# A delta rule and a SoLU layer in one kernel: an issue order for all engines written by hand, the first recurrence on GpSimd, weights on VectorE, 1/norm by Newton steps, softmax a step later

## The chip, the cores and the metric

The kernel runs on one core of one Trainium2 chip. The metric is device time in microseconds (us) of one execution. The engines are TensorE (PE in the profile, its weight loads PEld), VectorE (DVE), ScalarE (ACT), GpSimd (POOL) and SyncE (SP, which issues DMAs). Each works through its own queue in order, and they meet through semaphores.

## The reference

Inputs: q, k, v of shape (4 batches, 8 heads, 768 positions, 48), beta of shape (4, 8, 768), and the weights of a SoLU layer.

```python
k_n = k / (norm(k) + 1e-6)
state = zeros(B, H, D, D)
for t in range(768):
    y[t] = q[t] @ state
    v_old = state.T @ k_n[t]
    state = state + beta[t] * outer(k_n[t], v[t] - v_old)
x = y as (3072 tokens, 384)
h = x @ w_in                                  # 1024 columns
e = exp(h - max(h));  solu = h * e / (sum(e) + 1e-9)
ln = (solu - mean) / sqrt(var + 1e-6) * g_ln
out = ln @ w_out                              # 384 columns
```

## The kernel before

The delta rule is worked in chunks of 64 positions. A unit (bp, s, c2) is one pair of batches (bp), one of six blocks of 128 positions (s) and one half of it (c2): 24 units, walked by the loop `for n in range(N + 3)` with s outermost and bp innermost, so that the state of a pair of batches is used in every second step. For each block s, the four units' 32 x 32 Gram matrices are inverted together, with one matrix a partition: `inv_step` does a multiply (L269) and an add (L273) for each of 30 columns, on DVE for s = 0 and on POOL for the others. This is the recurrence ("rec s" below). It needs the Gram matrices (`gram_p` on PE, L180 and L183, copied by ACT, L196, and through DRAM and back by `to_inv`, tile gd and then ginv), the norms of the keys (`norms`, with a power on POOL, L224) and `inv_begin`. `inv_end` sends the inverse through DRAM into zt and gx (for s = 0 by DVE transposes, L278 and L280), and `tlevel_a`/`tlevel_b` (PE L309, L325; ACT L316, L331) join the 32-blocks to 64.

One step n of the chain: `chain_bank` (PE L352, state times k and q; DVE L354), `chain_ups` (PE L366, ACT L368), `chain_kpu` (PE L381 and L383; DVE L390 adds to the state, ACT L392 copies y). Behind the chain comes the layer: `moe_x` transposes y of unit n-1 and splits it in two f16 parts (PE L402, ACT L405, DVE L406), `moe_h` multiplies with w_in (18 matmuls, L415) and does the softmax and the normalization (DVE maximum L421, ACT exp L424, DVE product L426, ACT square L430, DVE L431 to L433, POOL power L434 and L435, ACT L436), `moe_p` transposes unit n-2 (PE L446, ACT L448, DVE L449) and `moe_o` multiplies unit n-3 with w_out (24 matmuls, L459).

PSUM holds one buffer for bank, ups and kpu in turn (tag "ch"), one for yps, one for h, two for Gram and tlevel work (tag "g") and two for the layer's other work. The weights come as 64-bit floats and are turned to two f16 parts by `split_w` (L94 to L102), w_in with POOL's help and w_out on DVE.

The order on PE is the order of the program, under this line; the other engines' instructions are put in order by a scheduler with a model of their costs:

```python
with tc.manual_schedule(engines={mybir.EngineType.PE}):
```

Of the kernel before, what the change touches and what calls it, by code (L numbers as in the profile page):

```python
# [622 lines left out]
```

## Time and profile before

| | us |
|---|---|
| median of 3 runs (lowest, highest) | 655.91 (655.41, 658.05) |
| the profiled execution | 655.79 |
| its span, first to last instruction | 654.1 |
| PE / DVE / ACT / POOL busy | 452.3 / 260.5 / 236.5 / 280.9 |
| mean granted clock of TensorE | 0.778 of 2.4 GHz |

In the rows that follow, a time is counted from the first instruction of the span. The granted clock is given as a share of 2.4 GHz; it takes two levels here, 1.00 (2.4 GHz) and 0.50 (1.2 GHz), so a value between them is a mix over the stretch. "A <- B" in a wait means that A's engine sat idle until B was done.

### The profile page before, as it was taken

The page shows a single profiled execution, that of the slowest core. Times are in us where ns is not written, and L with a number is a line of the kernel's source. Part 1 is how long each engine was busy: PE and PEld are TensorE (multiplying, and loading weights), DVE is VectorE, ACT ScalarE, POOL GpSimd, SP SyncE. Part 2 cuts the span into 40 slices and gives each one's busy share as a digit, 9 for nine tenths or more (in the row PEclk, how much of TensorE's full clock was granted, in tenths as well). Part 3 has the DMA queues.
Part 4 walks back from the last instruction along what each step waited for, and adds up shares of the span by engine and source line. Part 5 has one row for each costly group of instructions (what it writes and reads, how often), then busy time and mean ns, then how long its engine had stood idle before and what let it go on. Part 6 is the DMA issues. An engine that isn't in the chain of part 4 may idle for free.

```text
span 654.1 us, 18470 instructions
## 1 busy us (share of the span) xinstructions
PE 452.3 (69%) x8248; PEld 312.5 (48%) x8248; DVE 260.5 (40%) x516; ACT 236.5 (36%) x442; POOL 280.9 (43%) x418
## 2 busy tenths in 40 slices
PE   6430033819487869769859669848768888998975
PEld 5430033616354546536646446625445555655543
DVE  1789999121530432313441232343123332223341
ACT  2232152333332433243434244333153443424342
POOL 5786357864785038840048830068810000000000
PEclk9755555567697797777788788968967889878898
DMA  7963430128113532234232244311060000000000
GB/s 212 298 166 122 88 106 27 66 82 144 59 39 106 134 62 63 74 99 121 74 47 66 71 111 110 82 37 43 34 149 2 14 15 13 15 13 14 13 14 24
DMA packets 78159, 49.52 MB, mean 76 GB/s; under 512 B 64768, under 2 KB 67968, under 8 KB 78080
## 3 DMA queue, kind: packets, MB, share of 16 engines
q1 hardware_dynamic: 74624, 43.63, 25.9%
q10 hardware_dynamic: 3456, 4.72, 2.1%
q8 instruction: 64, 1.05, 0.7%
q14 instruction: 15, 0.12, 0.1%
HBM read 33.13 MB, written 15.20 MB: 74 GB/s over the span
## 4 chain that ended last, share of the span: by engine, by line
issue 42%; POOL 32%; DVE 11%; DMA 8%; SPq 4%; ACT 2%; PE 1%; POOLq 0%; DVEq 0%
POOL y L273 11%; POOL itmp L269 11%; POOL nn L224 3%; DVE y L273 3%; DMA ginv<-gd 3%; DVE itmp L269 2%; POOL y L254 2%; POOL st L434 2%; POOL v L243 2%; SPq L138 1%; DMA g_sb<-g_ln_dram 1%; DMA gd<-g 1%; SPq L209 1%; DMA kq<-kq_dram 1%; POOL y L255 1%
## 5 line engine op out<-in xcount | busy, mean ns | idle before, releaser
L434 POOL TENSOR_TENSOR st<-st,nhalf 128x1 f32<-128x1 f32 x24 | 13.2, 549 | 244.2 <-DVE st L433 244.2
L421 DVE TENSOR_REDUCE st<-h 128x1 f32<-128x1024 f32 x24 | 29.4, 1224 | 184.7 <-PE h L415 184.7
L352 PE MATMUL bank<-st,kq 48*64 48x48 f32 x704 | 39.5, 284 | 82.9 <-DVE st L390 69.6
L273 POOL TENSOR_TENSOR y<-y,itmp 128x30 f32<-128x30 f32 (+9 forms) x150 | 78.1, 521 | 10.9
L269 POOL TENSOR_TENSOR itmp<-y,ginv 128x30 f32<-128x30 f32 (+9 forms) x150 | 73.6, 490 | 10.8
L352 PEld LDWEIGHTS bank<-st,kq 48*64 48x64 f32 x704 | 36.3, 199 | 87.5 <-issue 72.5
L180 PE MATMUL p<-kq 48*64 48x64 f32 x768 | 48.8, 307 | 28.9 <-ACT pt L187 19.2
L459 PEld LDWEIGHTS <-ph 128*128 128x128 f16 x384 | 47.6, 124 | 42.9 <-issue 28.3
L459 PE MATMUL ops<-wout_hi,ph 128*128 128x384 f16 x192 | 57.8, 472 | 2.2 <-DVE st L422 1.1
L180 PEld LDWEIGHTS p<-kq 48*64 48x64 f32 x768 | 44.6, 216 | 30.2 <-ACT pt L187 19.9
L224 POOL TENSOR_TENSOR nn<-ginv,half 128x32 f32<-128x32 f32 x6 | 32.8, 5461 | 53.4 <-DMA ginv<-gd 47.1
L426 DVE SCALAR_TENSOR_TENSOR pr<-h,e 128x1024 f32<-128x1024 f32 x24 | 29.4, 1224 | 54.7 <-ACT e L424 54.7
L309 PE MATMUL mps<-zt,gx 32*32 32x32 f32 x768 | 19.2, 206 | 45.5 <-DVE zt L278 30.7
L436 ACT ACTIVATE pr<-pr,st 128x1024 f32<-128x1024 f32 x24 | 29.8, 1241 | 56.8 <-POOL st L435 56.8
L406 DVE TENSOR_TENSOR xl<-xps,xh 128x384 f16<-128x384 f32 x24 | 13.4, 557 | 84.7 <-ACT xh L405 84.4
L415 PEld LDWEIGHTS <-xh 128*128 128x128 f16 x288 | 28.4, 105 | 36.8 <-issue 11.0
L352 PE MATMUL yps<-st,kq 48*64 48x48 f32 x704 | 38.8, 285 | 9.1 <-ACT yo L392 9.1
L331 ACT COPY zt<-mps 32x256 f32<-32x256 f32 x48 | 17.4, 362 | 75.6 <-PE mps L325 75.3
L183 PE MATMUL g<-kq 48*64 48x64 f32 x640 | 38.4, 308 | 5.8 <-DVE pt L190 3.7
L415 PE MATMUL h<-win_hi,xh 128*128 128x512 f16 x144 | 41.4, 431 | 0.9 <-ACT xh L405 0.9
L430 ACT ACTIVATE e<-pr,st 128x1024 f32<-128x1024 f32 x24 | 27.6, 1149 | 39.2 <-DVE st L429 37.6
L352 PEld LDWEIGHTS yps<-st,kq 48*64 48x64 f32 x704 | 35.4, 199 | 9.4 <-ACT yo L392 9.4
(99 smaller groups left out, 990.5 us busy)
## 6 DMA issues: line engine op xcount, KB each, us to landing
kq<-kq_dram SPq DMA_DIRECT2D x40, 192.0 KB, 5.1
gd<-g SPq DMA_DIRECT2D x10, 512.0 KB, 2.8
v<-vn_dram SPq DMA_DIRECT2D x12, 384.0 KB, 4.5
k<-kn_dram SPq DMA_DIRECT2D x12, 384.0 KB, 3.8
out_dram<-o ACTq DMA_DIRECT2D x24, 192.0 KB, 1.9
wi<-w_in_dram SPq DMA_DIRECT2D x6, 512.0 KB, 7.2
wo<-w_out_dram SPq DMA_DIRECT2D x8, 384.0 KB, 3.1
ginv<-gd SPq DMA_DIRECT2D x20, 128.0 KB, 3.8
```

The costliest lines, as they stand in the source:

```text
L180: nc.tensor.matmul(out=ps[o : o + C, h], lhsT=k[lan, 0, h], rhs=k[lan, 1, h], start=True, stop=True)
L183: nc.tensor.matmul(out=gp[o : o + C, h], lhsT=k[lan, 0, h], rhs=k[lan, 0, h], start=True, stop=True)
L224: nc.gpsimd.tensor_tensor(out=n, in0=gi.rearrange("p j i -> p (j i)")[:, 0 : 32 * 32 : 33], in1=half, op=ALU.pow)
L269: eng.tensor_tensor(out=tv, in0=y[:, 0:j, j : j + 1].to_broadcast([P, j, n]), in1=b[:, j : j + 1, j + 1 : 32].to_broadcast([P, j, n]), op= ...
L273: eng.tensor_tensor(out=y[:, 0:j, j + 1 : 32], in0=y[:, 0:j, j + 1 : 32], in1=tv, op=ALU.add)
L352: nc.tensor.matmul(out=ps[o : o + C, h], lhsT=k[lan, i, h], rhs=sb[lan, h], start=i == 0 or h == 0, stop=i == 0)
L415: nc.tensor.matmul(out=hps[:, 512 * q : 512 * q + 512], lhsT=a[:, k], rhs=b[:, k, 512 * q : 512 * q + 512], start=j == 0, stop=j == len(pa ...
L421: nc.vector.tensor_reduce(out=nmax, in_=hps, op=ALU.max, axis=AX.X, negate=True)
L426: nc.vector.scalar_tensor_tensor(out=pr, in0=hps, scalar=1.0, in1=e, op0=ALU.mult, op1=ALU.mult, accum_out=sp,)
L430: nc.scalar.activation(e, pr, AF.Square, bias=mean, scale=1.0, accum_out=ss)
L436: nc.scalar.activation(pr, pr, AF.Identity, bias=mean, scale=rr)
L459: nc.tensor.matmul(out=ops, lhsT=a[:, k], rhs=b[:, k], start=i == 0, stop=i == 23)
```

## The change

All five engines now issue in the order of the program text, which is written out anew, for the stretch ahead of the loop and for each step. The loads stand first, in an order of their own. `inv_step` works on POOL for every s, and the loop takes rec s in three steps of ten columns, half of them at the step's start and half later, where it took two steps of fifteen. `inv_begin` becomes `inv_bm`, `inv_ya` and `inv_yb`. `norms` has no power on POOL: it takes 1/norm from an integer guess and three Newton steps on DVE. The weights are converted by DVE and ACT alone, with one DVE operation fewer, the last eight slices inside steps 0 to 2. The softmax of unit n-2 stands in step n, where `moe_h` of the same unit ran in step n-1; the last three of nine passes of `moe_h` go to the step's end, and `chain_kpu` stands ahead of `moe_p`. The output's DMA goes from ACT's queue to SP's. Buffers change by one here and there (pt 10 to 11, raw weights and pr 4, ginv 2, u and r 1).

```diff
-    p3 = ctx.enter_context(tc.tile_pool(name="p3", bufs=3))
+    pw = ctx.enter_context(tc.tile_pool(name="pw", bufs=4))
-    pm = ctx.enter_context(tc.tile_pool(name="pm", bufs=10))
+    pm = ctx.enter_context(tc.tile_pool(name="pm", bufs=11))
+    ctx.enter_context(tc.manual_schedule())
...
-            eng.tensor_scalar(out=c, in0=c, scalar1=(1.125 * 2.0**-15) ** 2, scalar2=by, op0=ALU.is_ge, op1=ALU.mult)
-            eng.tensor_tensor(out=u, in0=u, in1=c, op=ALU.mult)
-        nc.scalar.copy(out=hi_out, in_=u)
-        eng.tensor_tensor(out=lo_out, in0=u, in1=hi_out, op=ALU.subtract)
+            nc.vector.scalar_tensor_tensor(out=u, in0=c, scalar=(1.125 * 2.0**-15) ** 2, in1=u, op0=ALU.is_ge, op1=ALU.mult)
+        nc.scalar.mul(out=hi_out, in_=u, mul=by)
+        nc.vector.scalar_tensor_tensor(out=lo_out, in0=u, scalar=by, in1=hi_out, op0=ALU.mult, op1=ALU.subtract)
...
-        if pool:
-            nc.scalar.copy(out=pt, in_=ps)
-            nc.gpsimd.tensor_tensor(out=pt, in0=pt, in1=mk, op=ALU.mult)
-        else:
-            nc.vector.tensor_tensor(out=pt, in0=ps, in1=mk, op=ALU.mult)
+        nc.vector.tensor_tensor(out=pt, in0=ps, in1=mk, op=ALU.mult)
...
-        nc.gpsimd.tensor_tensor(out=n, in0=gi.rearrange("p j i -> p (j i)")[:, 0 : 32 * 32 : 33], in1=half, op=ALU.pow)
+        nc.vector.tensor_copy(out=x, in_=ginv[s].rearrange("p j i -> p (j i)")[:, 0 : 32 * 32 : 33])
+        nc.vector.tensor_scalar(out=t.bitcast(I32), in0=x.bitcast(I32), scalar1=1, scalar2=None, op0=ALU.logical_shift_right)
+        nc.vector.tensor_scalar(out=n.bitcast(I32), in0=t.bitcast(I32), scalar1=-1.0, scalar2=float(0x5F3759DF), op0=ALU.mult, op1=ALU.add)
+        for _ in range(3):
+            nc.vector.tensor_tensor(out=t, in0=x, in1=n, op=ALU.mult)
+            nc.vector.scalar_tensor_tensor(out=t, in0=t, scalar=-0.5, in1=n, op0=ALU.mult, op1=ALU.mult)
+            nc.vector.scalar_tensor_tensor(out=n, in0=t, scalar=1.5, in1=n, op0=ALU.add, op1=ALU.mult)
+        nc.vector.tensor_tensor(out=n, in0=n, in1=x, op=ALU.mult)
...
+    def inv_bm(s):
+        gi, nb = ginv[s], nbt[s]
+        nb_c = nb.unsqueeze(1).to_broadcast([P, 32, 32])
+        nc.vector.scalar_tensor_tensor(out=gi, in0=gi, scalar=-1.0, in1=nb_c, op0=ALU.mult, op1=ALU.mult)
+        nc.vector.memset(gi.rearrange("p j i -> p (j i)")[:, 0 : 32 * 32 : 33], 1.0)
+        bm[s] = gi
+
+    def inv_ya(s):
+        y = p1.tile([P, 32, 32], F32, tag="y", name=f"y_{s}")
+        nc.gpsimd.affine_select(
+            out=y, in_=nbt[s].unsqueeze(2).to_broadcast([P, 32, 32]), compare_op=ALU.is_ge, fill=0.0, base=0,
+            pattern=[[-1, 32], [1, 32]], channel_multiplier=0,
+        )
+        yt[s] = y
+
+    def inv_yb(s):
+        nc.vector.tensor_tensor(out=yt[s], in0=yt[s], in1=bm[s], op=ALU.mult)
...
-        eng = nc.vector if s == 0 else nc.gpsimd
+        eng = nc.gpsimd
...
-        nc.scalar.dma_start(out=out[bp, s, c2], in_=o)
+        nc.sync.dma_start(out=out[bp, s, c2], in_=o)
...
+    gram_0()
+    norms(0)
+    inv_ya(0)
+    inv_bm(0)
+    inv_yb(0)
+    inv(0, 1, 31)
+    gram_0x()
+    for bp in range(2):
+        fill_v(bp, 0, nc.vector)
+    for k in range(4):
+        gram_p(*unit(0, k))
+    conv_w(0)
+    conv_w(1)
+    for k in range(4):
+        gram_p(*unit(1, k))
+    to_inv(1)
+    to_gx(1)
+    load_w(4)
+    load_w(5)
+    conv_w(2)
+    conv_w(3)
+    load_w(6)
+    load_w(7)
+    norms(1)
+    inv_bm(1)
+    for bp in range(2):
+        fill_v(bp, 1, nc.vector)
+    conv_w(4)
+    conv_w(5)
+    scale_g()
...
+    inv_end_0()
+    inv_ya(1)
+    inv_yb(1)
+    inv(1, 1, 31)
...
+    for n in range(N + 3):
+        s, k = n // 4, n % 4
+        live, mx, mo, mp = n < N, 0 <= n - 1 < N, 0 <= n - 3 < N, 0 <= n - 2 < N
+        t, a = (n + 5) // 4, (n + 5) % 4
+        rec = t if 2 <= t < NS and a < 3 else None
+        if live:
+            chain_bank(n)
+        if mp:
+            sm_max(n - 2)
+        if live:
+            chain_r(n)
+        if mp:
+            sm_exp(n - 2)
+        if rec:
+            inv(rec, 10 * a + 1, 10 * a + 6)
...
+            m = n + 10
+            if m < N:
+                gram_p(*unit(m // 4, m % 4))
+                if m % 4 == 3:
+                    to_inv(m // 4)
+        if n % 4 == 2 and 1 <= (n + 2) // 4 < NS:
+            inv_end((n + 2) // 4)
...
+        if mp:
+            sm_pr(n - 2)
+            sm_square(n - 2)
+            sm_z(n - 2)
+        if mo:
+            moe_o(n - 3)
+        if mp:
+            sm_var(n - 2)
+        if mo:
+            moe_out(n - 3)
+        if mx:
+            moe_x(n - 1)
+        if mp:
+            sm_ln(n - 2)
+        if n < 3:
+            for i in range(3 * n, min(3 * n + 3, 8)):
+                conv_w(6 + i)
+                if i < 4:
+                    load_w(10 + i)
+        if n % 4 == 2 and 2 <= (n + 6) // 4 < NS:
+            norms((n + 6) // 4)
+            inv_ya((n + 6) // 4)
+            inv_bm((n + 6) // 4)
+        if live:
+            chain_ups(n)
+        m = n + 2 if n < 2 else n + 1
+        tl = m < N and n != 2
+        if tl:
+            tlevel_a(*unit(m // 4, m % 4))
+        if rec:
+            inv(rec, 10 * a + 6, 10 * a + 11)
+        if n % 4 == 2 and 2 <= (n + 2) // 4 < NS:
+            for bp in range(2):
+                fill_v(bp, (n + 2) // 4, nc.gpsimd)
+        if n % 4 == 2 and 2 <= (n + 6) // 4 < NS:
+            inv_yb((n + 6) // 4)
+        if mx:
+            moe_h(n - 1, 0, 6)
+        if tl:
+            tlevel_b(*unit(m // 4, m % 4))
+        if live:
+            chain_kpu(n)
+        if mp:
+            moe_p(n - 2)
+        if mx:
+            moe_h(n - 1, 6, 9)
```

## Rows read from the trace of the kernel before

**Rows 1.** The page's part 4, the chain that ended last, shares of the span by engine.

```profile
issue 42%; POOL 32%; DVE 11%; DMA 8%; SPq 4%; ACT 2%; PE 1%; POOLq 0%; DVEq 0%
```

**Rows 2.** Busy time by stretch: from:to, length, then PE, PEld, DVE, ACT and POOL busy us (instructions), the mean granted clock, DMA share and GB/s. First rec 0, the loop's steps 3 to 13, 14 to 22, and 23 to the end; then step 13 up to its last transposes, and the whole of step 19.

```profile
34.85:78.80 43.95, 6.97 (x191) 5.94 (x190) 42.27 (x75) 10.03 (x19) 29.05 (x22) 0.50 0.44 119
...
173.22:434.98 261.76, 202.59 (x3751) 139.02 (x3752) 83.47 (x187) 97.46 (x181) 124.73 (x206) 0.81 0.32 82
434.98:607.31 172.33, 144.39 (x2397) 95.51 (x2397) 56.28 (x122) 69.33 (x130) 41.09 (x82) 0.86 0.11 32
607.31:654.10 46.79, 34.66 (x291) 20.05 (x290) 14.17 (x33) 18.29 (x31) 2.21 (x6) 0.93 0.05 18
410.44:425.32 14.88, 14.88 (x341) 10.32 (x341) 4.41 (x9) 5.77 (x11) 1.67 (x3) 1.00 0.41 93
536.05:555.55 19.50, 16.97 (x277) 11.10 (x278) 6.57 (x16) 7.83 (x15) 0.74 (x2) 0.83 0.04 12
```

**Rows 3.** Who waited for whom over the whole span: total us, times, longest us.

```profile
PE bank L352 <- DVE st L390: 69.6, 20, 10.8
```

**Rows 4.** The timeline of DVE at the end of step 18: start, duration, engine, line, operation, out<-in and shapes; in brackets the idle time before and what ended it.

```profile
530.89 1.22 DVE L421 TENSOR_REDUCE st<-h 128x1 f32<-128x1024 f32 x1 [8.16 <-PE h L415]
...
533.58 1.22 DVE L426 SCALAR_TENSOR_TENSOR pr<-h,e 128x1024 f32<-128x1024 f32 x1 [1.27 <-ACT e L424]
...
534.79 1.11 DVE L390 TENSOR_TENSOR st<-st,kpu 48x384 f32<-48x384 f32 x2
...
537.73 0.21 DVE L433 TENSOR_SCALAR st<-st 128x1 f32<-128x1 f32 x1 [0.21 <-ACT e L430]
```

**Rows 5.** The timelines of ACT and of POOL in the same stretch.

```profile
532.34 1.11 ACT L424 ACTIVATE e<-h,st 128x1024 f32<-128x1024 f32 x1
...
536.46 1.15 ACT L430 ACTIVATE e<-pr,st 128x1024 f32<-128x1024 f32 x1 [1.57 <-DVE st L432]
...
538.88 1.24 ACT L436 ACTIVATE pr<-pr,st 128x1024 f32<-128x1024 f32 x1 [1.18 <-POOL st L435]
...
538.02 0.55 POOL L434 TENSOR_TENSOR st<-st,nhalf 128x1 f32<-128x1 f32 x1 [17.52 <-DVE st L433]
```

**Rows 6.** The timeline of PE in step 13 at the granted clock 1.00; a block's start to the next block's start is what it costs.

```profile
412.85 1.46 PE L459 MATMUL ops<-wout_hi,ph 128*128 128x384 f16 x8
...
416.84 1.14 PE L366 MATMUL ups<-r,zt 64*64 64x48 f32 x32
417.91 0.69 PE L309 MATMUL mps<-zt,gx 32*32 32x32 f32 x32
418.53 1.47 PE L415 MATMUL h<-win_hi,xh 128*128 128x512 f16 x6
```

**Rows 7.** Busy time by stretch as in rows 2: one unit's Gram work at the clock 0.50, the same at 1.00, and PE's idle time at the end of step 13.

```profile
44.50:46.96 2.46, 2.44 (x64) 2.06 (x64) 2.29 (x6) 0.43 (x1) 2.38 (x2) 0.50 0.00 0
...
411.42:412.47 1.05, 1.05 (x77) 0.98 (x68) 1.00 (x3) 0.99 (x2) 0.00 (x0) 1.00 0.00 0
...
425.32:434.98 9.66, 0.00 (x0) 0.03 (x1) 4.79 (x14) 2.55 (x5) 5.67 (x2) 0.74 0.10 16
```

**Rows 8.** Groups of instructions by line: shapes, count, busy us, mean ns of one, idle before.

```profile
L273 POOL TENSOR_TENSOR y<-y,itmp 128x30 f32<-128x30 f32 (+9 forms) x150 | 78.1, 521 | 10.9
L269 POOL TENSOR_TENSOR itmp<-y,ginv 128x30 f32<-128x30 f32 (+9 forms) x150 | 73.6, 490 | 10.8
...
L224 POOL TENSOR_TENSOR nn<-ginv,half 128x32 f32<-128x32 f32 x6 | 32.8, 5461 | 53.4 <-DMA ginv<-gd 47.1 <-DVE ginv L153 6.3
...
L316 ACT ACTIVATE msb<-mps 32x256 f32<-32x256 f32 x48 | 17.9, 373 | 6.4 <-PE mps L325 2.0 <-PE mps L309 1.9
...
L368 ACT COPY u<-ups 128x384 f32<-128x384 f32 x24 | 11.5, 478 | 16.2 <-PE ups L366 12.8 <-DMA xd<-ginv 2.2 <-ACT o L462 1.2
...
L190 DVE TENSOR_TENSOR pt<-p,mask 128x512 f32<-128x512 f32 x16 | 11.0, 690 | 5.2 <-PE yps L383 4.8
...
L252 DVE TENSOR_TENSOR ginv<-ginv,nn 128x1024 f32<-128x1024 f32 x6 | 7.3, 1220 | 0.1
```

**Rows 9.** The timeline of DVE ahead of the loop: the first Gram transpose; a weight operation of 512 columns; the transpose into zt; a small operation of `norms`; a weight operation of 384 columns while POOL stands still, and one while POOL works on rec 1.

```profile
10.14 1.93 DVE L153 STREAM_TRANSPOSE ginv<-dg 128x1024 f32<-128x1024 f32 x1 [10.14 <-PE dg L151]
...
53.60 0.68 DVE L97 SCALAR_TENSOR_TENSOR wf_i<-wi,wf_i 128x512 int32<-128x512 int32 x1
...
78.80 1.91 DVE L278 STREAM_TRANSPOSE zt<-y 128x1024 f32<-128x1024 f32 x1
...
90.93 0.17 DVE L225 TENSOR_SCALAR nn<-nn 128x32 f32<-128x32 f32 x1
...
91.48 0.55 DVE L97 SCALAR_TENSOR_TENSOR wf_o<-wo,wf_o 128x384 int32<-128x384 int32 x1
...
110.61 0.78 DVE L97 SCALAR_TENSOR_TENSOR wf_o<-wo,wf_o 128x384 int32<-128x384 int32 x1
```

**Rows 10.** The timeline of POOL: the same operation of rec 1 beside DVE's weight operations, and of rec 4 without them.

```profile
110.35 0.63 POOL L273 TENSOR_TENSOR y<-y,itmp 128x130 f32<-128x130 f32 x1
...
348.30 0.43 POOL L273 TENSOR_TENSOR y<-y,itmp 128x130 f32<-128x130 f32 x1
```

**Rows 11.** The chain that ended last, in order of time, in step 5: start, us, what. The Gram matrices of block 3 go out to DRAM and come back.

```profile
226.69 3.02 DMA gd<-g
...
231.31 4.07 DMA ginv<-gd
```

More of the change, by code (lines that the diff above doesn't have):

```diff
@@ L69 @@
         )
-    half = cp.tile([P, 32], F32, name="half")
-    nc.gpsimd.memset(half, 0.5)
+    ident = cp.tile([P, P], F32, name="ident")
+    make_identity(nc, ident)
     nhalf = cp.tile([P, 1], F32, name="nhalf")
     nc.gpsimd.memset(nhalf, -0.5)
+    zt = []
+    for i in range(2):
+        zt.append(cp.tile([P, 4 * H, C], F32, name=f"zt_{i}"))
+        for r0 in (32, 96):
+            nc.gpsimd.memset(zt[i][r0 : r0 + 32, :, 0:32], 0.0)
     bt = cp.tile([P, NS, 32], F32, name="bt")
@@ L318, in tlevel_b @@
     def tlevel_b(bp, s, c2):
-        zz, gx = zt[s % 2], gxt[s]
+        zz, gx = zt[s % 2], gxt[s] if s else x0[0]
         z0 = 2 * H * bp + H * c2
@@ L417, in moe_h, with sm_max @@
                     start=j == 0, stop=j == len(passes) - 1,
                 )
+    def sm_max(n):
         sm = p2.tile([P, 8], F32, tag="st", name=f"st_{n}")
-        nmax, z, sp, mean, ss, t0, var, rr = (sm[:, i : i + 1] for i in range(8))
-        nc.vector.tensor_reduce(out=nmax, in_=hps, op=ALU.max, axis=AX.X, negate=True)
+        sv[n] = [sm[:, i : i + 1] for i in range(8)]
+        nmax = sv[n][0]
+        nc.vector.tensor_reduce(out=nmax, in_=hp[n], op=ALU.max, axis=AX.X, negate=True)
@@ L435, in moe_h, with sm_ln @@
         nc.gpsimd.tensor_tensor(out=mean, in0=mean, in1=rr, op=ALU.mult)
-        nc.scalar.activation(pr, pr, AF.Identity, bias=mean, scale=rr)
-        pro[n] = pr
+    def sm_ln(n):
+        mean, rr = sv[n][3], sv[n][7]
+        nc.scalar.activation(pro[n], pro[n], AF.Identity, bias=mean, scale=rr)
     def moe_p(n):
@@ new lines @@
+    for k in range(4):
+        load_kq(*unit(0, k), slice(0, 1))
+    nc.sync.dma_start(out=bt, in_=beta)
+    for k in range(4):
+        load_kq(*unit(0, k), slice(1, 2))
+    for bp in range(2):
+        load_v(bp, 0)
+    for i in range(2):
+        load_w(i)
+    for k in range(4):
+        load_kq(*unit(1, k))
+    for i in range(2, 4):
+        load_w(i)
+    for bp in range(2):
+        load_k(bp, 0)
+    load_g()
+    for k in range(3):
+        load_kq(*unit(2, k))
+    for bp in range(2):
+        load_k(bp, 1)
+        load_v(bp, 1)
@@ new lines @@
+    conv_w(4)
+    conv_w(5)
+    scale_g()
+    load_w(8)
+    load_w(9)
+    inv_end_0()
+    inv_ya(1)
+    inv_yb(1)
+    inv(1, 1, 31)
+    for k in range(2):
+        tlevel_a(*unit(0, k))
+    for k in range(2):
+        tlevel_b(*unit(0, k))
+    for k in range(2):
+        gram_p(*unit(2, k))
+    for n in range(N + 3):
[14 more added lines that the diff above has]
+        if live:
+            if n + 11 < N:
+                load_kq(*unit((n + 11) // 4, (n + 11) % 4))
+            if k < 2 and 1 <= s < NS - 1:
+                load_k(k, s + 1)
+                load_v(k, s + 1)
+            m = n + 10
[5 more added lines that the diff above has]
+            inv_end((n + 2) // 4)
+        if n % 4 == 3 and 2 <= (n + 5) // 4 < NS:
+            to_gx((n + 5) // 4)
+        if mp:
[30 more added lines that the diff above has]
+        if n % 4 == 2 and 2 <= (n + 2) // 4 < NS:
+            for bp in range(2):
+                fill_v(bp, (n + 2) // 4, nc.gpsimd)
[5 more added lines that the diff above has]
+            tlevel_b(*unit(m // 4, m % 4))
+        if live:
+            chain_kpu(n)
[3 more added lines that the diff above has]
+            moe_h(n - 1, 6, 9)
```

249 lines of the change are left out of this document (88 added, 161 removed).

## The prediction

> **What bounds the kernel now.** I read the chain of waits first: 42% of it is "issue", PE working through its own queue, and 32% POOL [rows 1]. Then the stretches [rows 2]: steps 3 to 13 of the loop take 261.76 us (23.8 each) with PE busy for 203, steps 14 to 22 take 172.33 (19.1 each) with 144. So PE is the busiest engine but never full, and its granted clock is 0.81 and 0.86 there. The waits say for whom it stands: the next bank waits 69.6 us in 20 times for the addition to the state, L390 [rows 3]. The timeline of one step says why [rows 4]: that addition stands on DVE behind the maximum (from 530.89) and the product L426, which itself waits 1.27 us for ACT's exp. The softmax of unit n-1, which nobody on the chain needs, sits between kpu and the state. It also costs clock: step 19, which begins after such a wait, has a mean clock of 0.83 and takes 19.50 us, while step 13 up to its last transposes runs at 1.00 (2.4 GHz) in 14.88 us, all of it PE busy [rows 2]. After a longer idle stretch of PE the mean clock is 0.74 [rows 7].
>
> The rest of the span is the stretch ahead of step 3, 173.2 us: rec 0 on DVE takes 43.95 of it [rows 2], then rec 1 runs on POOL.
>
> **The change part by part: the loop.** Softmax n-2 moves to step n, next to matmuls that don't depend on it, and kpu's addition stands on DVE directly behind kpu. What PE does in a step is 14.88 us with Gram work at full clock, and 13.8 without (its Gram unit is 1.05) [rows 2, 7]. Is anything else late? One step in us from its bank: bank and Gram to 2.0; w_out 4.0, to 6.0; x transposed 6.4; ups 1.07, to 7.5; tlevel 0.6, to 8.1; two thirds of h, 2.7, to 10.8; tlevel 11.4; kpu 12.5; transposes 13.6; the last third of h 14.9 (h is 4.0 in three parts of six matmuls) [rows 6]. Beside it: maximum to 1.5, exp with its accumulator to 2.9, product 4.2, square to 5.6 and variance to 5.8, POOL's two operations to 6.7 [rows 4, 5]; on ACT then the copy of o, x (to 7.1), the normalization 1.24 to 8.3, u 0.48 to 8.8, tlevel's copies 2 x 0.37 to 9.6 [rows 5, 8]. Each is there before PE needs it: x at 7.1 for 8.1, tlevel's copies at 9.6 for 10.8, u for 11.4. The addition to the state ends at 13.7, the next bank comes at 14.9. Without Gram work the smallest reserve is 0.7. POOL has a rec third, 35.1 / 3 = 11.7 (thirty times 0.521 + 0.490 and 0.16 between [rows 8]; the middle third about 14), and 0.8 of softmax: it fits, in the middle third just so. So PE binds, the 2.5 us wait goes, the clock stays at 2.4 GHz, and next late is tlevel's copy.
>
> Steps 6, 10 and 14 are different. After xl (8.3) DVE has the norms, 18 operations of 0.17 and some 0.05 between [rows 9], 4.0; `inv_bm` and, one after the other since both use SBUF, POOL's select, 1.2 each (1.22 for this size [rows 8]), to 14.8; `inv_yb` 1.2 and part of a wait for POOL's `fill_v`, to 16.8; only then the state's 1.1 [rows 4], to 18. That is a stall of 3 us where POOL's power of 5.46 us [rows 8] went, and the clock falls after it: I add 2.5 to the next step (step 19's 19.50 against 13.8 and its wait of 2.5 leaves 3.2). Bounds: no stall, 14.9 (-6 for the pair), or each small operation waiting for a POOL operation of 0.6, +5. The Gram matrices' way through DRAM, 3.0 + 1.6 + 4.1 [rows 11], is issued a step earlier and hidden.
>
> Steps 3 to 13: 17.9 (step 3, cold) + 6 x 14.9 + 2 x (18 + 17.4) = 178.1. Steps 14 to 22: 17.6 + 16.3 + 7 x 13.8 = 130.5. Step 23 and the end: step 23 has no tlevel work, 12.5; in step 24 the transposes wait for the normalization at 8.4, to 11; step 25 9.5; then two splits 1.6, 24 matmuls partly at 1.2 GHz 5.5 (4.0 to 8.0), copy and output 2.5, rounded up to 43 against 46.79 [rows 2].
>
> **Ahead of the loop.** The first transpose ends at 12.07 [rows 9]. Norms 4.0, and three operations of 1.2 that exclude each other: rec 0 begins at 19.7 (34.85 before). On POOL it takes 35.1 and what DVE costs it. Beside DVE's weight operations a POOL operation takes 0.63 for 0.43 [rows 10], and DVE's takes 0.78 for 0.55 [rows 9]: about 0.2 to 0.3 each. With some 35 such operations rec 0 ends near 64. But `inv_end_0` stands on DVE behind a long queue: `fill_v` 2 x 1.2 (by size from 1.22, and the wait), masks 4 x 0.69 [rows 8], slices 0 and 1 (0.42, 3 x 0.98, ACT's 0.72, 0.98: 5.1 each from 0.68 [rows 9] and 0.3) 10.3, four masks of block 1 at PE's pace of 2.46 at 1.2 GHz [rows 7] 10.5, slices 2 and 3 10.3, norms and what follows 9.5, slices 4 and 5 undisturbed 7.8, two transposes of 1.91 [rows 9] and the g scale 4.1: 57.7, so 77.5. POOL idles for 13 us, and rec 1 runs from 80 to 123 (before 106 to 143).
>
> Then PE: tlevel work and three Gram units with their masks, 14 (3 x 3.15 and about 4.5), to 91.5; step 0 with three weight slices that stand on ACT ahead of u, 3 x 4.6 (0.35, 3 x 0.83, 0.6, 0.85, again with 0.3 for rec 1) and 6 for u, tlevel, kpu at half clock and copies, to 111; step 1 the same and 2 for x, to 133; step 2: softmax to xl 9, two clean slices 6.6, norms 4, 2.4 of `inv_bm` and `inv_yb`, state 1.1, to 156.4. So step 3 begins 17 us earlier. Bounds: without contention 20 x 0.3 on DVE's first queue and 24 x 0.3 in the steps go, and some waits, -20; if each operation waits for a whole one of the other engine (0.6 instead of 0.3), +15. I keep 0.3, which the rows show.
>
> The GPSIMD Engine Reference of the Trainium skill (section Engine selection) speaks against rec 0 on POOL: an elementwise operation with two inputs is about twice as slow there as on VectorE. By it rec 0 would take 88 us for 43.95, end at 108 instead of before 77, and the sum would be 34 us more, 544; the trace's 35.1 us for the same recurrence on POOL [rows 8] disagrees with the step from 43.95, because DVE's time holds other work and waits.
>
> **Sum.** 156.4 + 178.1 + 130.5 + 43 = 508; the execution is 1.7 longer than its span (655.79 against 654.1), and within 0.1 us of the median: 510 us.
>
> **Rivals.** (a) Contention, about 538: DVE's operations with two SBUF inputs and rec 0 and 1 exclude each other in full, also during the norms, +15 ahead of step 3 and 13 in the loop. For: both engines' operations grow beside each other [rows 9, 10]. Against: by 0.2, not by 0.5. Whether this counts shows ahead of the loop. The GPSIMD Engine Reference (Key points) says that the two share SBUF interfaces and names such operations; it gives no size.
>
> (b) A new wait in the strict order, about 605: POOL's power comes behind half a rec third (up to 7 us), ACT's normalization waits for it, and u and tlevel's copies stand behind that on ACT. With a reserve of 0.7 to 1.2 us, a delay of 3.5 brings back a PE wait of 2.5 and the clock's 2.5: 5 us in some 19 steps, +95. For: the small reserve and POOL's full middle third. Against: it can catch up in the steps without a rec.
>
> (c) Ahead of the loop and in steps 6, 10, 14 the waits are hidden, 470: -20, -18 and -2.
>
> (d) Slower: PE, now without pauses, is held at 1.2 GHz through the loop. Steps cost 2 x 14.4 on average, 20 of them 575 where I count 309, with the rest 156 + 575 + 60: about 790. It decides from a mean clock below 0.64, where the step passes 22.5 us. Against: step 13 at 1.00 without a pause [rows 2]; pauses go before every fall that I see.
>
> (e) The written order isn't what the queues get, or h's single buffer makes PE wait as before: 655.
>
> **Chances.** Forecast 0.58 (its own range 485 to 535), (a) 0.13, (b) 0.15, (c) 0.09, (d) 0.03, (e) 0.02. The range of 468 to 575 holds the forecast, (a), most of (c) and the mild part of (b). 0.5% is about what a measurement can tell from no change. Faster 0.95: all but (d) and (e); same 0.02; slower 0.03.
>
> **What would show it.** Right: the wait of bank for L390 shrinks from 69.6 to about 15 us, most of it in steps 2, 6, 10 and 14; the clock in the other steps is 1.00 and their length 13.8 to 14.9; rec 0 on POOL begins near 20 and its last operation ends well ahead of DVE's transpose into zt near 76; step 3's bank near 156. Wrong: PE waits in most steps for ACT (u or tlevel's copies), rec 0's end releases the transpose, or the loop's clock stays below 0.9.

## The result, and the profile after

The changed kernel takes 500.09 us (median of 4 runs, 497.68 to 501.2) against 655.66 (4 runs, 655.35 to 658.05) in the same comparison: a ratio of 0.7616, 95% interval 0.7583 to 0.765. The forecast was 510, with a range of 468 to 575. The profiled execution took 499.87, its span is 498.2 us, the mean granted clock 0.962 (0.778 before). Where one execution of six took over 1.5% longer than the fastest (experiments 3 and 4), the times given are those of the other five.

First the page of the changed kernel: busy time by engine, and the chain that ended last [rows 1].

```profile
PE 397.9 (80%) x8248; PEld 277.3 (56%) x8248; DVE 266.4 (53%) x554; ACT 229.6 (46%) x430; POOL 242.3 (49%) x436
...
PE 32%; issue 30%; DVE 17%; POOL 12%; ACT 4%; DMA 3%; SPq 1%; POOLq 0%; DVEq 0%; ACTq 0%
```

POOL's share of the chain fell from 32% to 12%, and PE's busy time fell too, from 452.3 to 397.9 us, though its instructions are the same in number: that is the clock, which in the loop rose from 0.81 and 0.86 [rows 2] to 0.98 and 0.99. Busy time by stretch, columns as in [rows 2]: rec 0, steps 3 to 13, 14 to 22, 23 to the end, then steps 7, 11 and 17 alone.

```profile
19.77:63.03 43.26, 12.29 (x320) 11.16 (x320) 30.41 (x52) 7.20 (x12) 38.63 (x60) 1.00 0.74 208
...
150.76:323.59 172.83, 166.06 (x3752) 115.44 (x3752) 94.70 (x209) 93.74 (x178) 109.18 (x205) 0.98 0.49 122
323.59:452.97 129.38, 126.08 (x2462) 85.00 (x2462) 65.17 (x146) 73.08 (x137) 45.42 (x83) 0.99 0.22 55
452.97:498.20 45.23, 35.05 (x291) 20.77 (x290) 15.29 (x34) 17.57 (x29) 2.21 (x6) 0.89 0.05 18
214.24:230.63 16.39, 16.39 (x341) 10.87 (x341) 8.06 (x17) 8.19 (x16) 11.82 (x27) 0.90 0.25 55
278.45:293.21 14.76, 14.76 (x341) 10.32 (x341) 8.06 (x17) 8.19 (x16) 10.37 (x25) 1.00 0.26 60
370.08:383.90 13.82, 13.82 (x278) 9.39 (x277) 6.59 (x15) 7.71 (x15) 9.54 (x22) 1.00 0.15 55
```

PE is busy for 166.06 of the 172.83 us of steps 3 to 13, where it was 202.59 of 261.76 [rows 2]. Against the stretches of before and the forecast (step 3 begins at 150.76):

| stretch | before | forecast | after |
|---|---|---|---|
| ahead of step 3 | 173.2 | 156.4 | 150.8 |
| steps 3 to 13 | 261.8 | 178.1 | 172.8 |
| steps 14 to 22 | 172.3 | 130.5 | 129.4 |
| step 23 to the end | 46.8 | 43 | 45.2 |
| span | 654.1 | 508 | 498.2 |

So 132 of the 156 us come from steps 3 to 22 of the loop, 22.5 from the stretch ahead of them. Who waited for whom, as [rows 3]:

```profile
PE mps L334 <- DVE zt L297: 28.9, 1, 28.9
...
PE mps L350 <- ACT msb L341: 19.9, 4, 13.2
...
POOL y L270 <- DVE x L300: 12.6, 1, 12.6
...
PE bank L377 <- DVE st L421: 11.6, 4, 3.3
```

The wait of bank for the state (now L377 and L421) went from 69.6 us in 20 times to 11.6 in 4. POOL stands 12.6 us after rec 0 for DVE's transposes (L297, L300), so DVE's queue binds ahead of the loop (experiments 5 and 8 test it). DVE's timeline shows why four waits are left and the others gone, first at the end of step 6, then of step 17 [rows 4]:

```profile
203.75 0.56 DVE L437 TENSOR_TENSOR xl<-xps,xh 128x384 f16<-128x384 f32 x1 [0.53 <-ACT xh L436]
204.22 0.18 DVE L235 COPY nx<-ginv 128x32 f32<-128x32 f32 x1
...
208.20 1.21 DVE L264 SCALAR_TENSOR_TENSOR ginv<-ginv,nb 128x1024 f32<-128x1024 f32 x1
...
210.57 2.49 DVE L277 TENSOR_TENSOR y<-y,ginv 128x1024 f32<-128x1024 f32 x1 [0.97 <-POOL y L270]
212.98 1.11 DVE L421 TENSOR_TENSOR st<-st,kpu 48x384 f32<-48x384 f32 x2
...
381.69 1.12 DVE L421 TENSOR_TENSOR st<-st,kpu 48x384 f32<-48x384 f32 x2 [4.58 <-PE yps L414]
382.89 1.29 DVE L501 TENSOR_TENSOR pl<-pps,ph 128x512 f16<-128x512 f32 x2
384.10 1.21 DVE L456 TENSOR_REDUCE st<-h 128x1 f32<-128x1024 f32 x1
```

In step 17 DVE idles until kpu is done, adds at once, and the maximum comes 2.4 us later, in the next step. In step 6 the norms (204.22 to 208.2), `inv_bm` and `inv_yb` stand between xl and the addition, and PE waits 2.79 us.

### The profile page after: what moved, and what is told of

The parts are those of the page before. It is cut to its first block, busy times and chain, and to the rows that moved or that the text cites. A ratio compares the mean times of both kernels' runs of the same rounds, so it can differ in the third digit from the quotient of the medians.

```text
span 498.2 us, 18513 instructions
## 1 busy us (share of the span) xinstructions
PE 397.9 (80%) x8248; PEld 277.3 (56%) x8248; DVE 266.4 (53%) x554; ACT 229.6 (46%) x430; POOL 242.3 (49%) x436
## 4 chain that ended last, share of the span: by engine, by line
PE 32%; issue 30%; DVE 17%; POOL 12%; ACT 4%; DMA 3%; SPq 1%; POOLq 0%; DVEq 0%; ACTq 0%
PE ops L511 8%; PE h L447 6%; POOL y L290 4%; POOL itmp L286 3%; PE p L191 3%; DMA zd<-y 2%; DVE wf L98 2%; DVE wf L99 2%; PE mps L350 2%; POOL y L270 2%; DVE wf L100 2%; PE g L194 2%; PE ups L397 2%; PE pps L498 2%; PE bank L377 2%
## 5 line engine op out<-in xcount | busy, mean ns | idle before, releaser
L290 POOL TENSOR_TENSOR y<-y,itmp 128x30 f32<-128x30 f32 (+9 forms) x180 | 98.7, 548 | 14.1
L286 POOL TENSOR_TENSOR itmp<-y,ginv 128x30 f32<-128x30 f32 (+9 forms) x180 | 94.1, 523 | 16.7 <-DVE y L277 4.0
L421 DVE TENSOR_TENSOR st<-st,kpu 48x384 f32<-48x384 f32 x40 | 22.1, 551 | 76.9 <-PE yps L414 76.7
L462 ACT ACTIVATE e<-h,st 128x1024 f32<-128x1024 f32 x24 | 26.7, 1113 | 70.9 <-DVE st L457 70.9
L191 PE MATMUL p<-kq 48*64 48x64 f32 x768 | 39.0, 271 | 14.9 <-ACT g L203 7.8
L501 DVE TENSOR_TENSOR pl<-pps,ph 128x512 f16<-128x512 f32 x48 | 31.0, 686 | 20.9 <-ACT ph L500 19.5
L334 PE MATMUL mps<-zt,gx 32*32 32x32 f32 x768 | 17.9, 200 | 28.9 <-DVE zt L297 28.9
L511 PE MATMUL ops<-wout_hi,ph 128*128 128x384 f16 x192 | 39.0, 350 | 1.1 <-DVE pl L501 0.5
L447 PE MATMUL h<-win_hi,xl 128*128 128x512 f16 x144 | 37.4, 398 | 0.0
L447 PE MATMUL h<-win_lo,xh 128*128 128x512 f16 x144 | 36.9, 395 | 0.0
L511 PE MATMUL ops<-wout_lo,ph 128*128 128x384 f16 x192 | 36.8, 337 | 0.0
L467 DVE SCALAR_TENSOR_TENSOR pr<-h,e 128x1024 f32<-128x1024 f32 x24 | 29.4, 1224 | 12.6 <-ACT e L462 11.8
L511 PE MATMUL ops<-wout_hi,pl 128*128 128x384 f16 x192 | 35.1, 326 | 0.0
L377 PEld LDWEIGHTS bank<-st,kq 48*64 48x64 f32 x704 | 22.9, 136 | 21.6 <-issue 21.6
```

The costliest lines, as they stand in the source:

```text
L191: nc.tensor.matmul(out=ps[o : o + C, h], lhsT=k[lan, 0, h], rhs=k[lan, 1, h], start=True, stop=True)
L286: eng.tensor_tensor(out=tv, in0=y[:, 0:j, j : j + 1].to_broadcast([P, j, n]), in1=b[:, j : j + 1, j + 1 : 32].to_broadcast([P, j, n]), op= ...
L290: eng.tensor_tensor(out=y[:, 0:j, j + 1 : 32], in0=y[:, 0:j, j + 1 : 32], in1=tv, op=ALU.add)
L377: nc.tensor.matmul(out=ps[o : o + C, h], lhsT=k[lan, i, h], rhs=sb[lan, h], start=i == 0 or h == 0, stop=i == 0)
L421: nc.vector.tensor_tensor(out=st[bp][lan], in0=st[bp][lan], in1=kps[lan], op=ALU.add)
L447: nc.tensor.matmul(out=hp[n][:, 512 * q : 512 * q + 512], lhsT=a[:, k], rhs=b[:, k, 512 * q : 512 * q + 512], start=j == 0, stop=j == len( ...
```

## The experiments

My theory: PE waited for an addition queued behind the softmax on DVE, and for the clock that fell behind each wait; with that gone PE binds, and small reserves on ACT, DVE and POOL hold it there. Ahead of the loop DVE's queue binds. The rivals: the order on PE alone does it; the place of the softmax counts little; rec 0 or the power has no part. Where no baseline is named, changes are against the 500.09 us.

**1. Softmax back in the same step.**

```diff
-            sm_max(n - 2)
...
-            sm_exp(n - 2)
...
-            sm_pr(n - 2)
-            sm_square(n - 2)
-            sm_z(n - 2)
...
-            moe_h(n - 1, 0, 6)
+            moe_h(n - 1, 0, 9)
+            sm_max(n - 1)
         if tl:
             tlevel_b(*unit(m // 4, m % 4))
+        if mx:
+            sm_exp(n - 1)
+            sm_pr(n - 1)
         if live:
             chain_kpu(n)
...
-            moe_h(n - 1, 6, 9)
+            sm_square(n - 1)
+            sm_z(n - 1)
```

A softmax in the same step needs the whole of h, so the last third of h moves ahead of kpu as well; what that costs by itself is experiment 4.

> The changed kernel, but the maximum, exp, product, square and z of unit n-1 stand in step n again, right behind its nine passes of h and ahead of kpu's addition on DVE; the order of all engines is still written by hand. Theory (the softmax on DVE's queue ahead of the addition is what PE waited for): PE's bank waits about 2.5 us for the addition in most of the 20 steps with h, and the clock falls behind it, as in the kernel before: steps near 18.8 without Gram work and 19.9 with it instead of 13.8 and 14.8, about 600 us in all (570 to 610). Rival (the hand order as such is the gain, and the place of the softmax counts little): steps grow by less than 2 us, under 540 us.

Measured: 609.96 us (605.34 to 609.99), 110 more, as the theory has it. The wait is back, and with it the loss of clock; the waits row, then step 21 by the columns of [rows 2]:

```profile
PE bank L377 <- DVE st L421: 73.1, 20, 10.8
```

```profile
521.85:541.30 19.45, 16.79 (x277) 10.94 (x278) 6.58 (x15) 7.50 (x17) 0.74 (x2) 0.84 0.03 13
```

Steps 14 to 22 take 171.5 us (385.17 to 556.69), as in the kernel before (172.33 [rows 2]); with Gram work a normal step takes 20.4. Of the 110 us 62 are this wait (73.1 less 11.6). Most of the rest is clock: in steps 3 to 22 PE is busy for 341.2 us instead of 292.1 with the same instructions. Against experiment 4, where h is whole too, the softmax's place alone makes 90 us. So the rival falls: the hand order with the softmax in the old place gives back more than half of the gain, and with h whole seven tenths.

**2. The kernel before, only PE's order changed: three forms.** First kpu and the transposes of unit n-2 ahead of h:

```diff
-            if 0 <= n - 1 < N:
-                moe_h(n - 1)
+            if 0 <= n - 2 < N:
+                moe_p(n - 2)
             if n < N:
                 if m < N:
                     tlevel_b(*unit(m // 4, m % 4))
                 chain_kpu(n)
-            if 0 <= n - 2 < N:
-                moe_p(n - 2)
+            if 0 <= n - 1 < N:
+                moe_h(n - 1)
```

> The kernel before, with one edit: in PE's written order of a step the transposes of unit n-2, tlevel's second half and kpu stand ahead of h of unit n-1 instead of behind it; DVE, ACT and POOL keep the scheduler's order. Theory (PE's 69.6 us behind the addition to the state is the loop's cost, whoever orders the other engines): the wait and the clock falls go, steps near 15 to 16.5, the stretch ahead of the loop stays, so 535 to 565 us. Rival (the scheduler then puts other work ahead of the addition, so that the hand order on DVE and ACT is needed): PE waits elsewhere, 620 us or more.

Measured: 621.64 us, 0.9512 (0.9445 to 0.958) of the kernel before: 31 us less, as the rival has it. The wait for L390 is gone, and another of its size is there:

```profile
PE pps L446 <- ACT pr L436: 71.2, 20, 12.7
```

That was partly the experiment's doing, since I had moved the transposes too. So kpu alone ahead of h, the transposes behind it:

```diff
-            if 0 <= n - 1 < N:
-                moe_h(n - 1)
             if n < N:
                 if m < N:
                     tlevel_b(*unit(m // 4, m % 4))
                 chain_kpu(n)
+            if 0 <= n - 1 < N:
+                moe_h(n - 1)
             if 0 <= n - 2 < N:
                 moe_p(n - 2)
```

> The kernel before, with one edit: in PE's written order of a step tlevel's second half and kpu stand ahead of h of unit n-1 instead of behind it; the transposes of unit n-2 stay behind h (in the run with the transposes ahead of h PE waited 71 us for their normalization instead of 70 us for the state, and that hid the answer). Theory (PE's wait for the addition to the state was the loop's cost, and an order on PE alone removes it): the wait goes, nothing takes its place, steps 15 to 17, 545 to 575 us in all. Rival (kpu then waits for u, which the scheduler puts on ACT behind the softmax, or the addition still stands behind the maximum on DVE, so that the hand order on DVE and ACT is needed): PE waits over 30 us for ACT or DVE, 600 us or more.

Measured: 660.91 us against 657.61, a ratio of 1.0055 (1.0034 to 1.0076): nothing won, the theory of this run fell. Its waits, and ACT's timeline in step 17:

```profile
PE mps L325 <- ACT msb L316: 74.6, 24, 16.3
...
PE bank L352 <- DVE st L390: 4.6, 2, 2.9
```

```profile
514.33 1.24 ACT L436 ACTIVATE pr<-pr,st 128x1024 f32<-128x1024 f32 x1 [0.81 <-POOL st L435]
...
515.48 0.46 ACT L368 COPY u<-ups 128x384 f32<-128x384 f32 x1
515.84 0.76 ACT L316 ACTIVATE msb<-mps 32x256 f32<-32x256 f32 x2
```

The 69.6 us became 4.6, but without h between tlevel's halves PE reaches the second half while ACT is still at the normalization; u and the copy stand behind it. More than half of the 74.6 us (9.0, 16.3 and 13.7) falls in steps 3, 7 and 11, where the normalization itself stood 7 to 11 us for POOL's power. Then PE's full order of the changed kernel, w_out ahead of x and the last third of h behind kpu:

```diff
+            if 0 <= n - 3 < N:
+                moe_o(n - 3)
             if 0 <= n - 1 < N:
                 moe_x(n - 1)
-            if 0 <= n - 3 < N:
-                moe_o(n - 3)
...
-                moe_h(n - 1)
+                moe_h(n - 1, 0, 6)
             if n < N:
                 if m < N:
                     tlevel_b(*unit(m // 4, m % 4))
                 chain_kpu(n)
             if 0 <= n - 2 < N:
                 moe_p(n - 2)
+            if 0 <= n - 1 < N:
+                moe_h(n - 1, 6, 9)
```

> The kernel before with PE's order of a step as in the changed kernel (w_out's product ahead of x, two thirds of h, tlevel's second half, kpu, the transposes of unit n-2, the last third of h), so that a softmax can only begin behind kpu; the scheduler keeps the order of DVE, ACT and POOL, and all else is as before. Theory (the hand order on the other engines is needed too): the scheduler puts ACT's and DVE's softmax work ahead of copies that PE waits for, PE's waits move and stay above 50 us in the loop, 600 us or more. Rival (the place of kpu against the softmax is all, and PE's order settles it): PE's waits in the loop fall under 30 us, 525 to 565 us.

Measured: 607.25 us, 0.9256 (0.9208 to 0.9303) of the kernel before: 49 of the 156 us. Waits, and ACT in step 20:

```profile
PE h L417 <- ACT xh L405: 48.7, 19, 6.9
...
PE bank L352 <- DVE st L390: 4.9, 1, 4.9
```

```profile
516.05 1.24 ACT L440 ACTIVATE pr<-pr,st 128x1024 f32<-128x1024 f32 x1 [0.80 <-POOL st L439]
...
517.20 0.46 ACT L405 CAST xh<-xps 128x384 f16<-128x384 f32 x1
```

Again ACT: the copy of x, which PE needs for h, stands behind the normalization. Step 20 takes 16.9 us instead of 13.82: 1.4 of wait for x, the rest clock.

**3. That one exchange in the changed kernel.**

```diff
-        if mx:
-            moe_x(n - 1)
         if mp:
             sm_ln(n - 2)
+        if mx:
+            moe_x(n - 1)
```

> The changed kernel, but two neighbours change places on ACT: the normalization of unit n-2 stands ahead of the copy of x of unit n-1 instead of behind it; nothing else moves. Theory (in the run with PE's order alone the loop's rest was ACT's copy of x behind the normalization, which waits for POOL's power): PE waits 1 to 2 us a step for the copy of x, the clock falls behind it, steps near 16.9 instead of 13.8 without Gram work and 17 to 20 instead of 14.8 with it, 545 to 575 us. Rival (what was left in that run came from the rest of the scheduler's order and the old places of recs and norms): PE's wait is under 0.3 us a step and the time under 515 us.

Measured: 534.72 us (532.19 to 538.8), 35 more, between the two expectations. The profiled execution took 541.62 us, so only its waits are read, not its clock:

```profile
PE h L447 <- ACT xh L436: 27.3, 19, 5.0
```

5.3 us in 2 times became 27.3 in 19. Two neighbours on ACT are worth 35 us, where I had looked for 45 to 75; in that the theory was too large. The last form of experiment 2 lies 107 us above the changed kernel: 18.5 of that stand ahead of step 3, this exchange is worth 35, and what the rest consists of was not taken apart.

**4. All of h ahead of kpu.**

```diff
-            moe_h(n - 1, 0, 6)
+            moe_h(n - 1, 0, 9)
...
-        if mx:
-            moe_h(n - 1, 6, 9)
```

> The changed kernel, but all nine passes of h stand ahead of tlevel's second half and kpu, none at the step's end; every other engine's order is as it is. Theory (PE binds and its work is the same; behind kpu there are 1.1 us of transposes, about what the addition takes): PE's bank waits 0.1 to 0.4 us a step for the addition, 500 to 507 us. Rival (the last third of h is the cover that hides the addition, and without it a wait of 0.5 us or more comes back with clock falls behind it): 512 us or more.

Measured: 519.52 us (515.47 to 520.96), 19 more: by the time, the rival.

```profile
PE bank L377 <- DVE st L421: 21.3, 20, 6.7
```

This wait grew by 9.7 us, 4.1 of them in step 2, though step 3 begins no later (150.81 for 150.76). In an ordinary step it is 0.28 us, as the theory had it, but steps 16 to 21 take 14.4 to 14.7 us instead of 13.82, PE waiting in them 0.2 to 0.4 us for x as well, and the mean clock is 0.943 for 0.962. The last third of h covers the addition, and more than the addition.

**5. Rec 0 on DVE.**

```diff
-        eng = nc.gpsimd
+        eng = nc.vector if s == 0 else nc.gpsimd
```

> The changed kernel, but the first recurrence (60 operations) runs on DVE, POOL idle meanwhile. Theory (DVE's queue ahead of the transposes into zt is what binds ahead of the loop, rec 0 on POOL ends 9 us earlier): DVE has some 60 x 0.40 = 24 us more in the queue, less what contention with POOL costs it now (some 30 operations x 0.2 to 0.3), so zt's transpose near 86 to 90 instead of 71.8, step 3's bank near 165 instead of 150.8, and 512 to 517 us. Rival (GpSimd is twice as slow on these operations and the contention costs more than the move brings): rec 0 ends early, zt comes no later, 500 us or less.

Measured: 514.36 us (513.36 to 514.89), 14 more, as the theory has it. One line's instructions ahead of the loop, durations as least/median/greatest ns: L290 is half the rec, L98 a weight operation. First the changed kernel, then the experiment.

```profile
L290 POOL TENSOR_TENSOR y<-y,itmp x30: 285/628/978, 20.7 to 62.1; 128x30 f32<-128x30 f32 x2, 128x58 f32<-128x58 f32 x2, 128x84 f32<-128x84 f32 x2, 128x108 f32<-128x108 f32 x2
...
L98 DVE SCALAR_TENSOR_TENSOR wf<-wi,wf x4: 920/951/1047, 27.0 to 51.6; 128x512 int32<-128x512 int32 x4
```

```profile
L98 DVE SCALAR_TENSOR_TENSOR wf<-wi,wf x4: 691/692/693, 48.8 to 69.6; 128x512 int32<-128x512 int32 x4
...
L290 DVE TENSOR_TENSOR y<-y,itmp x30: 191/350/407, 19.9 to 41.4; 128x30 f32<-128x30 f32 x2, 128x58 f32<-128x58 f32 x2, 128x84 f32<-128x84 f32 x2, 128x108 f32<-128x108 f32 x2
```

The rec takes 21.9 us on DVE (19.7 to 41.6) and 43.3 on POOL (19.8 to 63.0), and beside it each weight operation of DVE takes 0.26 us more. DVE's last transpose still ends 17.2 us later with the rec on DVE (92.7 for 75.5): about 22 us more in the queue, less what contention had cost. The GPSIMD Engine Reference of the Trainium skill (section Engine selection) says that elementwise work with two inputs is about twice as slow there. The trace agrees for the whole rec (43.3 us for 21.9), with DVE's weight operations beside POOL's; undisturbed, the smallest operation takes 0.23 us on POOL and 0.19 on DVE. The factor does not decide the time, since POOL had nothing else to do.

**6. The power on POOL again.**

```diff
-        nc.vector.tensor_copy(out=x, in_=ginv[s].rearrange("p j i -> p (j i)")[:, 0 : 32 * 32 : 33])
...
-        nc.vector.tensor_tensor(out=n, in0=n, in1=x, op=ALU.mult)
+        nc.gpsimd.tensor_tensor(out=n, in0=ginv[s].rearrange("p j i -> p (j i)")[:, 0 : 32 * 32 : 33], in1=half, op=ALU.pow)
```

> The changed kernel, but the norms take their power on POOL in one operation (5.5 us in the kernel before) in place of the 18 small DVE operations of 4 us. Theory (POOL's queue is in order and rec 0 stands ahead of the power of norms 1): norms 1 ends only near 63 + 5.5, so DVE's queue with the transposes into zt comes some 5 to 9 us later, and in steps 6, 10 and 14 the power's 5.5 us stands behind ten columns of a rec on POOL or adds to them: stalls there longer by 2 to 4 us each; in all 515 to 525 us. Rival (the power is hidden beside other work in the steps, and POOL idles ahead of the loop anyway): 498 to 504 us.

Measured: 514.82 us (513.75 to 515.86), 15 more. POOL's timeline at the end of rec 0, and DVE's:

```profile
63.75 0.26 POOL L284 TENSOR_TENSOR y<-y,itmp 128x30 f32<-128x30 f32 x1
63.96 5.46 POOL L236 TENSOR_TENSOR nn<-ginv,half 128x32 f32<-128x32 f32 x1
```

```profile
69.45 0.18 DVE L237 TENSOR_SCALAR nn<-nn 128x32 f32<-128x32 f32 x1 [10.59 <-POOL nn L236]
```

The transpose into zt begins at 81.5 instead of 71.8; step 3's bank is 6.7 us later (157.5), and the stalls of steps 6, 10 and 14 are 4.8 to 5.7 us instead of 2.8 to 3.3.

**7. Norms early.**

```diff
+        nb_step = n % 4 == 2 and 2 <= (n + 6) // 4 < NS
+        if nb_step:
+            norms((n + 6) // 4)
+            inv_ya((n + 6) // 4)
         if mx:
             moe_x(n - 1)
...
-            norms((n + 6) // 4)
-            inv_ya((n + 6) // 4)
...
-            inv_yb((n + 6) // 4)
...
         if live:
             chain_kpu(n)
+        if nb_step:
+            inv_yb((n + 6) // 4)
```

POOL's `fill_v` goes from steps 6, 10, 14 and 18 to the step behind each.

> The changed kernel, but in steps 2, 6, 10 and 14 the norms and POOL's select stand on DVE and POOL ahead of the layer's x instead of behind it, the product inv_yb behind the addition to the state instead of ahead of it, and POOL's fill_v one step later. Theory (the four stalls of 2.6 to 3.3 us are DVE's 18 small operations and inv_bm and inv_yb standing ahead of the state, and the clock falls of the steps behind belong to them): the stalls shrink to under 0.7 us, steps 6, 10 and 14 take 14.8 to 15.5 instead of 17.2 to 17.7 and steps 7 and 15 14.8 and 13.8, so 12 us (9 to 15) less, about 488 us. Rival (what is moved ahead of x makes xl or u late by the same 4 us, PE waits there): gain under 4 us.

Measured: 496.16 us (491.56 to 496.84), 4 less where 12 were expected. Steps 6, 10 and 14 take 15.1, 14.8 and 13.8: the stalls are gone as forecast. In step 2 the wait for the state is gone too, but PE waits 7.2 us for u instead of 3.2, as the rival has it, and the step is 1.1 us longer. And steps 8, 12 and 16 take 17.9, 16.5 and 18.2. POOL's timeline in steps 7 and 8, and ACT's in 8:

```profile
225.18 2.91 POOL L257 TENSOR_TENSOR v<-v,nrn 128x768 f32<-128x768 f32 x2
...
234.97 0.55 POOL L484 TENSOR_TENSOR st<-st,nhalf 128x1 f32<-128x1 f32 x1
235.60 0.19 POOL L485 TENSOR_TENSOR st<-st 128x1 f32<-128x1 f32 x1
```

```profile
235.83 1.24 ACT L489 ACTIVATE pr<-pr,st 128x1024 f32<-128x1024 f32 x1 [2.89 <-POOL st L485]
236.97 0.46 ACT L399 COPY u<-ups 128x384 f32<-128x384 f32 x1
237.33 0.76 ACT L341 ACTIVATE msb<-mps 32x256 f32<-32x256 f32 x2
```

`fill_v` set POOL's rec back by 2.9 us, the power came late, and the chain over ACT made PE wait 1.1 to 2.6 us for the copy: rival (b) of the prediction, brought about by 2.9 us on POOL.

**8. Two weight slices behind the transposes into zt.**

```diff
-    conv_w(4)
-    conv_w(5)
-    scale_g()
-    load_w(8)
-    load_w(9)
     inv_end_0()
...
     for k in range(2):
         gram_p(*unit(2, k))
+        conv_w(4 + k)
+    scale_g()
+    load_w(8)
+    load_w(9)
```

> The changed kernel, but the last two slices of w_in are converted on DVE behind the transposes into zt, one behind each of the two Gram units of block 2, instead of ahead of them. Theory (the transposes wait for DVE's queue alone: 8 us of the two slices and the scale, where rec 0 on POOL has been done since 63.0): zt's transpose near 64 instead of 71.8, rec 1 from 68, step 3's bank 5 to 8 us earlier, 492 to 495 us. Rival (the slices now stand ahead of steps 0 and 1, beside rec 1, and delay these by what was won): 498 to 503 us.

Measured: 495.8 us (494.5 to 500.32), 4 less; by the profile only 2.0 of it at step 3 (148.77), so nearer the rival. The rest lies behind step 22 (42.3 us for 45.2, at a clock of 0.96 for 0.89), which the edit doesn't touch. PE's wait for zt fell by 8.0 us, to 20.9, as the theory says, but the slices now run beside rec 1:

```profile
L98 DVE SCALAR_TENSOR_TENSOR wf<-wi,wf x2: 920/932/944, 76.3 to 82.1; 128x512 int32<-128x512 int32 x2
```

0.93 us for 0.69, and PE waits 9.9 us for DVE's masks where it waited 7.1, and for one more mask, which stands behind a slice, 3.0.

**9. Both edits together; and both with `fill_v` left in its place.** The second against the first:

```diff
-        if n % 4 == 3 and 2 <= (n + 1) // 4 < NS:
+        if n % 4 == 2 and 2 <= (n + 2) // 4 < NS:
             for bp in range(2):
-                fill_v(bp, (n + 1) // 4, nc.gpsimd)
+                fill_v(bp, (n + 2) // 4, nc.gpsimd)
```

> Both edits together: norms early in steps 2, 6, 10 and 14, and two slices of w_in behind the transposes into zt. Theory: the two lie in different stretches (steps 6 to 15, and ahead of step 3), so their gains add to within 2 us: about 480 us if each brings what is expected. Rival: they share step 2, where the first has less to gain once DVE's queue is fuller there: 3 to 6 us less than the sum.

> As the run with both edits, but POOL's fill_v stays in steps 6, 10 and 14, where the changed kernel has it, right behind the select. Theory (the new waits of tlevel's second half for ACT's copy in steps 8, 12 and 16, and the clock falls there, come from the 2.9 us of fill_v among POOL's rec columns in steps 7, 11 and 15: the power, then ACT's normalization, u and the copy come late): these waits go, steps 8, 12 and 16 take 14.8, 14.8 and 13.8 instead of 18.1, 16.5 and 18.1, about 483 us (480 to 486). Rival (they come from inv_yb behind the state, which starts the rec late): the waits stay, 490 us or more.

Measured: 492.51 us (489.8 to 495.15), within 1 us of the sum of the two gains; and 485.53 us (484.52 to 486.76), a ratio to the kernel before of 0.7419 (0.7388 to 0.7451), the fastest here. Steps 8, 12 and 16 then take 14.8, 15.65 and 13.8. Steps 3 to 13 and 14 to 22, columns as in [rows 2]:

```profile
148.12:312.59 164.47, 163.16 (x3753) 113.69 (x3752) 92.42 (x208) 93.96 (x178) 108.83 (x205) 1.00 0.50 128
312.59:438.43 125.84, 124.46 (x2463) 84.53 (x2462) 64.57 (x146) 73.06 (x137) 45.34 (x83) 1.00 0.23 56
```

No wait of bank for the state is left in the loop, PE works through 163.16 of 164.47 us at the full clock. That settles that `fill_v`, not `inv_yb` behind the state, had made the new waits.

## Why the prediction came out

**The bound of the loop: right, but half the story.** The softmax on DVE ahead of the state was what PE waited for (experiment 1 against 4). In four of the 20 waits it was not alone: 33.5 of the 69.6 us fall at the ends of steps 2, 5, 9 and 13 (10.8, 6.4, 6.7 and 9.7), where the norms stood on DVE among the softmax's operations and waited for POOL's power. DVE's timeline of the kernel before at the end of step 13:

```profile
429.87 0.18 DVE L225 TENSOR_SCALAR nn<-nn 128x32 f32<-128x32 f32 x1 [5.94 <-POOL nn L224]
429.96 0.14 DVE L422 TENSOR_SCALAR st<-st 128x1 f32<-128x1 f32 x1
...
433.73 1.11 DVE L390 TENSOR_TENSOR st<-st,kpu 48x384 f32<-48x384 f32 x2
```

ACT's exp needs the scaled maximum of L422, and the addition L390 came behind the product of that exp. So some of the gain in these waits is that of the norms' new form and place: 11.6 us are left of the 33.5, and with the power back on POOL (experiment 6) 15.8.

That the addition stands directly behind kpu is not enough: the PE orders of experiment 2 took that wait away too, and another came in its place, for the normalization, for tlevel's copy, for x. What the prediction called a reserve of 0.7 to 1.2 us (x at 7.1 for 8.1, the copies at 9.6 for 10.8) is where the gain would have gone: one exchange on ACT costs 35 us, h in one piece 19, 2.9 us on POOL in three steps 7 (492.51 instead of 485.53). The gain in the loop is that of the order on all engines together.

**The step: right.** Forecast 14.9 with Gram work and 13.8 without; measured 14.76 and 13.82, PE busy throughout; only steps 9 and 12 took more (15.4 and 15.6).

**Steps 6, 10 and 14: the mechanism right, the clock term too large.** Stalls of 2.79, 2.85 and 3.30 us for 3, steps of 17.65, 17.68 and 17.18 for 18, 18 and 17.6. The 2.5 us added to the step behind measured 1.63, 0 and 1.68 (16.39, 14.76 and 15.5). `inv_yb` took 2.49 us, its 1.2 and the rest beside `fill_v`, as counted. This term, in steps 7 and 11, makes 3.7 of the 5.3 us by which steps 3 to 13 were overestimated; step 3, 16.3 for 17.9, is another 1.6.

**Ahead of the loop: the path right, the end of it forecast 5.6 us too late.** Rec 0 ran from 19.8 to 63.0 (forecast 19.7 to 64), DVE's last transpose was done at 75.5 (77.5): 2.0 of the 5.6 us. Rec 1 ended at 117.0, not 123, and the slices of step 1, from 110.8 on, met little of it: 3.6 us each (a weight operation took 0.56 in two of three) where I had put 4.6, which makes 3.0 us for three. Step 2's bank came at 127.5 for 133, step 3's at 150.8 for 156.4. The term that was most off is "step 1 the same".

**Rec 0 on POOL: the right side, a wrong reason.** I set aside the factor of two that the Trainium skill gives (GPSIMD Engine Reference, section Engine selection), because 43.95 on DVE became 35.1 on POOL. Measured on the two engines, the rec takes 21.9 and 43.3 us. The rec's length did not matter, since DVE's queue ended later.

**The end: 45.2 for 43.** PE waits 2.19 us for x in step 24 and 4.19 for the last normalization, and the stretch's clock is 0.89; in experiment 8, with the same waits and the clock at 0.96, the stretch takes 42.3.

**The rivals.** (a) 538: contention on DVE's weight operations is 0.26 us, as forecast, not 0.5; a long operation grew by more beside another (`inv_yb`, 2.49 us for 1.2 beside `fill_v`), and that the forecast had counted. (b) 605: not in this kernel; experiments 3 and 7 show how close. (c) 470: the waits at steps 6, 10 and 14 were not hidden; the order that hides them gives 485.5. (d) 790: the clock is 0.98 and 0.99 in the loop. (e) fell with the first row of waits.

Not tried: DVE alone for the weights, the loads' new order and the output's queue by themselves.
